# Pooled attention and a mixer on one core: K and Q turned by VectorE, maxima and diagonal Q moved by DMA

## The chip, the cores and the metric

The kernel runs on one core of one Trainium2 chip. The metric is the device time of one execution in microseconds (us). Before the change it is 923.01 us, the median of three runs (922.84 to 927.38).

## What is computed

Four batches of eight heads of attention, then a mixer over the result. The queries are averaged in pairs first, so each head has 576 pooled queries and 1152 keys of 64 numbers.

```python
q_pool = q.reshape(B, H, S // 2, 2, D).mean(axis=3)
scores = scale * np.matmul(q_pool, k.transpose(0, 1, 3, 2))
scores = scores - np.max(scores, axis=-1, keepdims=True)
attn = np.exp(scores)
attn = attn / (np.sum(attn, axis=-1, keepdims=True) + 1e-09)
x = np.matmul(attn, v)               # heads side by side: 4 x 576 x 512
h = np.maximum(x.T @ w_tok1, 0) @ w_tok2     # token mix, per batch
u = x + h.T
out = u + np.maximum(u @ w_ch1, 0) @ w_ch2   # channel mix
```

## The kernel before

Precision comes from splitting. [...] Everything is written as steps with a cost, a due time and buffers; a list planner (`Plan.run`) replays them on a model of the engines and so fixes, once, the order of each engine's instructions. The due times stand in the table `DUE`, in units of which one head has nine (`NS`), and `AFTER` and the cost functions are the planner's prices.

Work is done by pairs of heads, because two heads of 64 fill 128 partitions:

- `load_kq` loads K and Q of a pair (SP's queue): K as nine chunks into `KN`, Q with the two members of each pooled pair into `QN`. `prep_kq` adds the two members (`QP`, GpSimd or VectorE, L577) and turns K and Q by TensorE: three 128x128 turns for each of three K thirds (L588), three and two for Q (L614), into a slot of the PSUM ring `r` of three. ScalarE copies the rounded part out of the slot (`KHI`, L597; `QHI`, L628), VectorE subtracts it for the rest (`KLO`, L602; `QLO`, L638). ScalarE also copies the last 64 queries of each head into a diagonal tile `QD` (L634).
- `stack` puts, by DMA, the parts of one head on top of each other (`QQ`, `KK`, L666; `K2`, `Q2`, L671 and L674), so one 128-row matmul makes two of the products.
- `maxima` finds the row maximum of each query: twelve matmuls a head of 128 queries by 384 keys into a ring slot (L726) and a VectorE reduce each (L728), plus three a pair for the diagonal. A last reduce (L690) gives `MH`; TensorE turns it (L697), ScalarE copies it (`MT`, L699), and two DMAs write it as row 64 of `Q2` (L701, L704), so the scores matmul subtracts the maximum by itself.
- `main` runs nine steps a head: four scores matmuls of 288 columns (L792), two exponentials on ScalarE (`pf` in full at L807 into `PF`, rounded `ph` at L810), the rest `pl` on GpSimd or VectorE (L814), and PV matmuls (L839). In the heads of `IN_PV` (16 of 32) V has a 65th column of ones, so PV delivers the denominator and takes three matmuls a unit instead of two. The other heads add up `PF` on VectorE (L821) and turn the sums on TensorE (L885).
- `finish` turns the output of a head (L877), with 65 rows in `IN_PV` heads and 64 in the others, and scales it into `U` (L906).
- `token_mix` runs after every fourth head (L937, L955). After the last head the channel mixer `mm3`, `mm4` (L1052, L1080) runs with weights that `load_ch` narrowed from 64-bit words.

Tokens of K and V lie so that partition p holds tokens 9p to 9p+8 (`"(p c) d -> p c d"`); K's order within a head is free as long as V has the same.

Of the kernel before, what the change touches and what calls it, by code (L numbers as in the profile page):

```python
# [25 lines left out]
    (ACT, DVE): 131, (DVE, ACT): 128, (ACT, POOL): 159, (POOL, ACT): 75,  # L26
# [7 lines left out]
    "scores": -2.94,  # L34
    "p_lo": 5.94,
    "sum": -8.53,
    "pv": 1.65,
    "o": -51.23,
    "finish": 9.59,
    "max": -26.45,  # L40
    "max_each": 0.91,
    "prep": -32.39,
    "v": 3.41,
    "stack": 10.93,
    "stack_2": 29.0,
    "mix": 4.49,
    "mix_x": 5.65,
    "w_tok": 9.27,
    "w_tok_each": 4.51,
    "w_bits": -133.66,  # L50
    "sum_each": 0.15,
    "pv_lo": 0.35,
    "lo_first": -20.44,
# [40 lines left out]
IN_PV = (0, 1, 2, 3, 5, 8, 10, 13, 15, 19, 21, 24, 26, 28, 29, 31)  # L94
# [147 lines left out]
def kernel(  # L242
# [78 lines left out]
    def pool_(n):  # L321
        return 175 + 2.1 * n
# [101 lines left out]
    QP = early.tile([P, NQ, 2, D], F32, name="qp")  # L424
    VN = fix.tile([P, NK, D], F32, name="vn")
# [7 lines left out]
    MT = many(fix, 2, [NQ, P], F32, "mt")  # L433
# [8 lines left out]
    ve.memset(f(MH), 0.0)  # L442
# [3 lines left out]
    po.memset(PF[:, :, NK // 2, :, 1], 0.0)  # L446
# [28 lines left out]
    def tok_weights(after):  # L475
# [19 lines left out]
        for i, c, wh, wl in (  # L495
# [8 lines left out]
            for k, o in enumerate(  # L504
# [16 lines left out]
                step(POOL, 150 + 1.1 * m, lambda tmp=tmp: po.tensor_scalar(  # L521
# [24 lines left out]
    def load_kq(p, t, after):  # L546
        b, h0 = divmod(2 * p, H)

        def load_k(j, c0, c1):
            step(DMA, 2 * wire(4 * P * (c1 - c0) * D), lambda: sy.dma_start(  # L550
                KN[:, c0:c1, j], k[b, h0 + j].rearrange("(p c) d -> p c d", c=NK)[:, c0:c1]),
                t, write=[("kn", j, c) for c in range(c0 // 3, c1 // 3)], after=after)

        def load_q(j, c0, c1):
# [16 lines left out]
    def prep_kq(p, t):  # L571

        qh, ql = QHI[p % 2], QLO[p % 2]
        for i, (c0, c1) in enumerate(((0, 2), (2, 4), (4, 5))):
# [4 lines left out]
                t + due["q_pool"], [("qn", j, i // 2) for j in range(2)], [("qp", i)])  # L579
        tq = t - 1 if p == 0 else t + due["q_turn"]  # L580

        def keys(j):
# [3 lines left out]
            def turn(ps=ps, j=j):  # L586
                for c in range(3):
# [4 lines left out]
            step(PE, 3 * TURN, turn, t + j * due["k_each"], [("kn", 0, j), ("kn", 1, j)],  # L592
                 [ps, ("kh", j), ("kl", j)], [ps])
# [12 lines left out]
        def queries(i):  # L606
# [5 lines left out]
            def turn(ps=ps, c0=c0, c1=c1):  # L612
                for c in range(c0, c1):
# [4 lines left out]
            step(PE, (c1 - c0) * TURN, turn, tq + i,  # L618
                 [("qp", x) for x in ((0, 1) if i == 0 else (1, 2))],
                 [ps, ("qh", p % 2, i), ("ql", p % 2, i),  # L620
                  *(("qd", p % 2, x) for x in range(2 * i))], [ps])
# [55 lines left out]
    def maxima(h, t):  # L677
# [513 lines left out]
```

## Time and profile before

| | |
|---|---|
| median of three runs | 923.01 us |
| the profiled execution | 922.62 us |
| its span on the core | 920.8 us |
| TensorE busy, share of the span | 889.5 us, 97% |
| VectorE, ScalarE, GpSimd busy | 590.7, 562.1, 512.0 us |
| granted clock of TensorE, mean | 0.994 |
| DMA packets | 89686, 91.09 MB |

The span runs from the first to the last instruction; the rest of the execution's time lies around it. Busy times are unions of instructions, and matmuls overlap, so a busy TensorE is not one at its peak: the distance between starts says more. A line such as `L588 PE MATMUL r<-ident,kn 128*128 128x128 f32 x141 | 23.0, 275` would read: line 588, TensorE, writes `r` from `ident` and `kn`, 141 times, 23.0 us busy in all, 275 ns each; PEld is TensorE's weight load, DVE VectorE, ACT ScalarE, POOL GpSimd. Idle time and its releaser follow, where shown.

### The profile page before, as it was taken

What the parts mean: (1) busy time and instruction counts of PE and PEld (TensorE: products, weight loads), DVE (VectorE), ACT (ScalarE), POOL (GpSimd) and SP (SyncE); (2) the same over time, 40 slices, a digit from 0 to 9 for tenths busy, and PEclk for the clock granted to TensorE, in tenths of its full rate; (3) what the DMA queues carried; (4) which work ended last, traced back from release to release, by engine and by line L of the source; (5) the groups of instructions that cost most, each with busy time, mean ns of one, the idle gap of its engine ahead of it and who ended that gap; (6) DMA issues with size and microseconds to landing.
All of it is one profiled execution on the core that took longest, in us unless ns stands there. A gap on an engine that the chain in (4) does not pass through costs nothing.

```text
span 920.8 us, 15741 instructions
## 1 busy us (share of the span) xinstructions
PE 889.5 (97%) x5601; PEld 811.3 (88%) x5601; DVE 590.7 (64%) x1142; ACT 562.1 (61%) x1202; POOL 512.0 (56%) x414
## 2 busy tenths in 40 slices
PE   8899999999999999999999999999999999999997
PEld 6778889899989898999889999889989999998996
DVE  7567878887887689697888865778872222121211
ACT  5669889698788788798788979764431111111110
POOL 3679999797797698788688768643330000000000
PEclk9899999999999999999999999999999999999999
DMA  7778564565455555546634532133420101000001
GB/s 163 213 174 183 116 152 109 124 142 136 110 124 129 124 123 130 135 96 150 143 72 110 109 92 79 46 108 124 136 92 27 43 1 35 1 35 1 35 0 35
DMA packets 89686, 91.09 MB, mean 99 GB/s; under 512 B 43852, under 2 KB 68808, under 8 KB 89608
## 3 DMA queue, kind: packets, MB, share of 16 engines
q1 hardware_dynamic: 89608, 90.09, 39.9%
q8 instruction: 44, 0.72, 0.3%
q14 instruction: 34, 0.28, 0.1%
HBM read 43.25 MB, written 4.72 MB: 52 GB/s over the span
## 4 chain that ended last, share of the span: by engine, by line
PE 75%; ACT 10%; DVE 5%; issue 2%; DMA 1%; POOL 1%; SPq 0%; ACTq 0%; DVEq 0%; POOLq 0%
PE r L1052 17%; PE o L839 14%; PE s L1080 13%; PE s L792 12%; PE r L726 7%; ACT pf L807 3%; ACT ph L810 3%; PE o L1080 3%; PE r L937 2%; PE r L955 2%; PE r L877 2%; DVE mx L728 1%; PE r L885 1%; ACT u L906 1%; PE r L588 1%
## 5 line engine op out<-in xcount | busy, mean ns | idle before, releaser
L814 POOL TENSOR_TENSOR pl<-pf,ph 128x576 fp32r<-128x576 f32 x264 | 377.4, 1447 | 93.2 <-ACT pf L807 38.9
L728 DVE TENSOR_REDUCE mx<-r 128x1 f32<-128x384 f32 x384 | 197.4, 548 | 41.6 <-PE r L726 37.9
L810 ACT ACTIVATE ph<-s 128x576 fp32r<-128x576 f32 x288 | 187.6, 655 | 50.8 <-PE s L792 38.9
L807 ACT ACTIVATE pf<-s 128x576 f32<-128x576 f32 x288 | 194.2, 680 | 9.4 <-POOL pl L814 7.1
L839 PE MATMUL o<-ph,vv 128*65 128x288 f32 (+2 forms) x864 | 186.9, 302 | 3.9 <-ACT ot L846 1.4
L792 PE MATMUL s<-qq,kk 128*128 128x288 f32 x574 | 170.4, 309 | 5.6 <-ACT pf L807 5.3
L792 PE MATMUL s<-q,k 65*128 65x288 f32 x576 | 165.0, 298 | 1.4 <-ACT q L761 1.4
L1058 ACT ACTIVATE h<-r 128x384 fp32r<-128x384 f32 x72 | 35.3, 491 | 194.1 <-PE r L1052 194.0
L1060 DVE SCALAR_TENSOR_TENSOR h<-r,h 128x384 fp32r<-128x384 f32 x72 | 40.1, 556 | 169.0 <-ACT h L1058 168.8
L839 PE MATMUL o<-pl,vv 128*65 128x288 f32 (+1 forms) x576 | 135.7, 297 | 0.2 <-POOL pl L814 0.2
L839 PEld LDWEIGHTS o<-ph,vv 128*65 128x65 f32 (+2 forms) x864 | 125.7, 155 | 11.1 <-DVE ot L852 3.0
L726 PE MATMUL r<-kk,qq 128*128 128x384 f32 x372 | 127.1, 361 | 6.7 <-DMA q<-ql 1.2
L1080 PE MATMUL s<-w,h 128*128 128x512 f32 x504 | 130.8, 394 | 0.0
L792 PEld LDWEIGHTS s<-qq,kk 128*128 128x128 f32 x574 | 109.4, 191 | 14.9 <-ACT pf L807 12.3
L792 PEld LDWEIGHTS s<-q,k 65*128 65x128 f32 x576 | 110.1, 191 | 1.6 <-ACT q L761 1.6
L1052 PE MATMUL r<-big,w 128*128 128x384 f32 x576 | 109.0, 337 | 0.0
L821 DVE TENSOR_REDUCE sum<-pf 128x96 f32<-128x960 f32 x96 | 108.0, 1141 | 1.5 <-ACT pf L807 1.2
L1080 PEld LDWEIGHTS s<-w,h 128*128 128x128 f32 x504 | 93.4, 188 | 16.5
L1052 PEld LDWEIGHTS r<-big,w 128*128 128x128 f32 x576 | 101.7, 188 | 3.6 <-DVE big L1041 0.2
L839 PEld LDWEIGHTS o<-pl,vv 128*65 128x65 f32 (+1 forms) x576 | 88.1, 163 | 1.8 <-POOL pl L814 0.6
L726 PEld LDWEIGHTS r<-kk,qq 128*128 128x128 f32 x372 | 68.1, 189 | 19.2 <-DVE mx L728 4.6
L1015 POOL TENSOR_TENSOR w<-v,w 128x512 fp32r<-128x512 f32 x23 | 32.1, 1396 | 58.1 <-ACT w L1014 58.1
(131 smaller groups left out, 1168.5 us busy)
## 6 DMA issues: line engine op xcount, KB each, us to landing
raw<-in_moe_w_ch_dram SPq DMA_DIRECT2D x24, 512.0 KB, 3.6
kk<-kh SPq DMA_DIRECT2D x32, 288.0 KB, 6.2
qq<-qh SPq DMA_DIRECT2D x64, 144.0 KB, 3.0
kk<-kl SPq DMA_DIRECT2D x32, 288.0 KB, 4.2
vn<-in_v_dram SPq DMA_DIRECT2D x32, 288.0 KB, 2.6
k<-kk SPq DMA_DIRECT2D x31, 288.0 KB, 4.4
kn<-in_k_dram SPq DMA_DIRECT2D x30, 288.0 KB, 4.5
qn<-in_q_dram SPq DMA_DIRECT2D x32, 256.0 KB, 5.5
```

Source lines behind the costliest of these rows:

```text
L726: step(PE, mm(SP3), lambda ps=ps, w=w, x=x: te.matmul(at(ps)[:, 0:SP3], w, x, start=True, stop=True), t, read, [ps], [ps])
L728: step(DVE, dve(SP3), lambda ps=ps, m=m: ve.tensor_reduce(m, at(ps)[:, 0:SP3], axis=AX.X, op=ALU.max), t + due["max_of"], [ps], [key])
L792: te.matmul(at(st)[:, i, 0:HF], w[:, c * P:(c + 1) * P], x[:, fq * HF:(fq + 1) * HF], start=(n == 0), stop=(n == len(terms) - 1))
L807: step(ACT, act_ps(2 * HF) + (0 if near else 49), lambda pf=pf, st=st: sc.activation(pf, at(st)[:, :, 0:HF], AF.Exp, scale=ESC), t, [(st, ...
L810: step(ACT, act_ps(2 * HF), lambda ph=ph, st=st: sc.activation(at(ph), at(st)[:, :, 0:HF], AF.Exp, scale=ESC), t + due["p_hi"], [(st, 0), ...
L814: both(2 * HF, lambda e, pf=pf, ph=ph, pl=pl: e.tensor_sub(at(pl), pf, f(at(ph))), t + due["p_lo"], [("pf", s), ph], [pl], [pl], on=POOL i ...
L821: step(DVE, 65 + 1.06 * (NK + 1) * HF // CUT, lambda fq=fq, cs=cs: ve.tensor_reduce(SUM[:, fq, cs], PF[:, fq, :, cs].rearrange("p c x i -> ...
L839: lambda o=o, x=x, w=w, m=m, i=i, c=c, new=new, end=end: te.matmul(at(o)[0:m - w], VV[i2][:, c, w:m], at(x)[:, i], start=new, stop=end),
L1052: te.matmul(at(ps)[:, 0:GT], w[:, c], x[:, c], start=(c == 0 and n == 0), stop=(c == NC4 - 1 and n == 2))
L1058: step(ACT, act_ps(GT), lambda: sc.activation(at(h)[:, 0], at(ps)[:, 0:GT], AF.Relu), t, [ps], [h])
L1060: step(DVE, dve(GT), lambda: ve.scalar_tensor_tensor(out=at(h)[:, 1], in0=at(ps)[:, 0:GT], scalar=0.0, in1=f(at(h))[:, 0], op0=ALU.max, op ...
L1080: te.matmul(at(ps), a[:, x * P:(x + 1) * P], w, start=(fi == 0 and m == 0), stop=(fi == NF - 1 and m == 2))
```

## The change

For all pairs but the first:

- K and Q come as pieces of 32 floats (128 bytes), so that each 32 partitions hold one half of a head's 64 numbers, tokens by blocks of 32. VectorE then turns blocks of 32x32 within these partitions, 384 or 192 columns an instruction, straight into the ring slot. The TensorE turns of these pairs go. K and V have tokens in natural order now.
- The diagonal `QD` is copied by DMA from `QHI` instead of by ScalarE from PSUM.

For all heads: `MH` is written to the row of `Q2` by DMA as it is, 128 pieces of four floats, without TensorE's turn and ScalarE's copy; for that, a maxima matmul takes every fourth query (`c:4*P:4`) as its weights. V comes in nine pieces of 256 bytes a partition. Nineteen heads are in `IN_PV`. The output turn always has 65 rows. `PF` has ten slots in a row, five a half; slot numbers shift and nothing else. Many due times and some planner prices differ, so the order does too.

```diff
-    (ACT, DVE): 131, (DVE, ACT): 128, (ACT, POOL): 159, (POOL, ACT): 75,
+    (ACT, DVE): 131, (DVE, ACT): 128, (ACT, POOL): 235, (PE, POOL): 200, (POOL, ACT): 75,
...
-    "max_row": -47.64,
+    "max_row": -21.2,
...
-    "prep": -32.39,
+    "prep": -47.86,
...
+    "q_diag": -18.19,
...
-IN_PV = (0, 1, 2, 3, 5, 8, 10, 13, 15, 19, 21, 24, 26, 28, 29, 31)
+IN_PV = (0, 1, 2, 3, 5, 8, 10, 12, 13, 14, 16, 18, 21, 22, 23, 24, 26, 27, 31)
...
+    KBF = KN.rearrange("p c j d -> p (c j d)")
+    KB = KBF.rearrange("p (m i) -> p m i", i=32)
...
+        def load_k_blocks(j, y):
+            g = slice(64 * j + 32 * y, 64 * j + 32 * y + 32)
+            step(DMA, 2.1 * wire(4 * S * 32), lambda: sy.dma_start(
+                KB[g], k[b, h0 + j].rearrange("(m r) (y i) -> y r m i", r=32, y=2)[y]),
+                t, write=[("kn", j, c, y) for c in range(3)], after=after)
+
+        def load_q_blocks(j, y, x):
+            g = slice(64 * j + 32 * y, 64 * j + 32 * y + 32)
+            step(DMA, 2.1 * wire(4 * SQ * 32), lambda: sy.dma_start(
+                QB[g, x], q[b, h0 + j].rearrange("(m r x) (y i) -> x y r m i", r=32, x=2, y=2)[x, y]),
+                t, write=[("qn", j, y, x)], after=after)
...
+        for i, (o0, o1) in enumerate(((0, 384), (384, SQ)) if p else ()):
+            both(o1 - o0, lambda e, o0=o0, o1=o1: e.tensor_add(
+                QPB[:, o0:o1], QBF[:, 0, o0:o1], QBF[:, 1, o0:o1]), t + due["q_pool"],
...
+                step(DVE, 1.2 * SP3, lambda ps=ps, o=o: ve.transpose(
+                    bank(ps)[:, 0:SP3], KBF[:, o]), t + j * due["k_each"] + due["k_turn"], read,
+                    [ps, ("kh", j), ("kl", j)], [ps])
...
+                step(DVE, 1.2 * n, lambda ps=ps, o=o, n=n: ve.transpose(
+                    bank(ps)[:, 0:n], QPB[:, o]), tq + i, [("qp", i)], write, [ps])
...
+                        step(DMA, 100, lambda r=r, j=j: sy.dma_start(
+                            f(QD[p % 2])[r, j * REM:(j + 1) * REM], f(qh)[r, SQ - REM:SQ]),
+                             tq + 1.1 + due["q_diag"], [("qh", p % 2, 1)], [("qd", p % 2, j)])
...
-             lambda: sy.dma_start(vn, v[h // H, h % H].rearrange("(p c) d -> p c d", c=NK)),
+             lambda: sy.dma_start(vn, v[h // H, h % H].rearrange("(c p) d -> p c d", p=P)),
...
-        ps = Buf("r")
-        step(PE, 56, lambda: te.transpose(fr(at(ps))[:, 0:P], mh, identr), t,
-             ["mh"], [ps], [ps])
-        step(ACT, 158, lambda: sc.copy(mt, at(ps)[0:NQ, 0:P]), t, [ps], [("mt", h % 2)])
         row = f(Q2[h % 2])[D:D + 1]
-        step(DMA, 1, lambda: sy.dma_start(row[:, 0:4 * P], mt[0:4]), t,
-             [("mt", h % 2)], [("row", h % 2, c) for c in range(4)])
+        step(DMA, 300, lambda: sy.dma_start(
+            row[:, 0:4 * P].rearrange("o (p c) -> o p c", c=4), mh[:, 0:4]), t,
+            [("mh", 0)], [("row", h % 2, c) for c in range(4)])
...
-                w, x = QQ[i3][:, qc(c)], KK[i3][:, ks]
+                w, x = QQ[i3][:, c:4 * P:4], KK[i3][:, ks]
...
-        n = DT if pv else D
         for c in range(NQ):
             step(PE, 64, lambda c=c: te.transpose(
-                turned()[:, c, 0:n], ot[0:n, qc(c)], ident[0:n, 0:n]),
+                turned()[:, c, 0:DT], ot[0:DT, qc(c)], ident[0:DT, 0:DT]),
```

TensorE in the fifth head (head 4), where its output is turned for `finish`; `r` are ring slots, `ot` the output, `sum` the sums of float parts, `kn` the K of a later pair. Before:

```order
L588 MATMUL r_82<-ident,kn 128x128 x3
L726 MATMUL r_80<-kk_90,qq_95 128x384
...
L877 MATMUL r_81<-ident,ot_103 128x64
L885 MATMUL r_81<-ident,sum 128x128
L885 MATMUL r_82<-ident,sum 128x128 x4
L877 MATMUL r_81<-ident,ot_103 128x64 x4
L726 MATMUL r_80<-kk_90,qq_95 128x384
```

And now:

```order
L824 MATMUL s_78<-q_98,k_93 128x288
L870 MATMUL o<-ph_149,vv_119 65x288
L870 MATMUL o<-ph_149,vv_119 64x288 x2
L870 MATMUL o<-ph_149,vv_119 65x288
L907 MATMUL r_82<-ident,ot_103 128x65
L915 MATMUL r_82<-ident,sum 128x128
L907 MATMUL r_82<-ident,ot_103 128x65 x4
L915 MATMUL r_80<-ident,sum 128x128 x4
L870 MATMUL o<-pl_155,vv_119 65x288 x2
```

The turns of `kn` are gone from TensorE, and the output turns among the sum turns have 65 rows.

VectorE in the same heads: what stands around the K rests (`kl`). Before:

```order
L728 TENSOR_REDUCE mx_121<-r_80 128x1
L728 TENSOR_REDUCE mx_121<-r_81 128x1
L602 TENSOR_TENSOR kl<-r_82,kh 128x384
L728 TENSOR_REDUCE mx_121<-r_80 128x1
L814 TENSOR_TENSOR pl_158<-pf,ph_152 128x576
```

And now:

```order
L760 TENSOR_REDUCE mx_121<-r_82 128x1
L619 STREAM_TRANSPOSE r_82<-kn 128x384
L760 TENSOR_REDUCE mx_121<-r_80 128x1
L619 STREAM_TRANSPOSE r_80<-kn 128x384
L883 TENSOR_TENSOR ot_103<-o,low 64x288
L630 TENSOR_TENSOR kl<-r_82,kh 128x384
L630 TENSOR_TENSOR kl<-r_80,kh 128x384
```

Each K third now has two instructions on VectorE, the turn into the slot and the subtraction out of it, with ScalarE's copy between.

SP's queue, from one pair's loads to the maxima row of the next head (`q_98` is `Q2`; `mt` and `mh` the maxima). Before:

```order
L550 DMA kn<-in_k_dram 128x9x64 x2
L704 DMA q_98<-mt_123 1x16x4
L666 DMA qq_94<-qh_115 64x576 x2
L666 DMA kk_89<-kh 64x1152
L666 DMA kk_89<-kl 64x1152
L671 DMA k_93<-kk_91 64x1152
L674 DMA q_98<-ql_116 64x576
L701 DMA q_98<-mt_124 1x4x128
```

And now:

```order
L563 DMA kn<-in_k_dram 32x36x32 x4
L732 DMA q_98<-mh 1x128x4
L701 DMA kk_90<-kh 64x1152
L701 DMA kk_90<-kl 64x1152
L669 DMA qd_101<-qh_115 64x64 x2
L684 DMA vn<-in_v_dram 128x9x64
L569 DMA qn<-in_q_dram 32x18x32 x8
```

K and Q of a pair are twelve transfers where they were six, and they stand between the stacking transfers and the rows of the heads in work.

## Rows read from the trace of the kernel before

**Rows 1.** The page, part 1: busy us (share of the span) and instructions.

```profile
PE 889.5 (97%) x5601; PEld 811.3 (88%) x5601; DVE 590.7 (64%) x1142; ACT 562.1 (61%) x1202; POOL 512.0 (56%) x414
```

**Rows 2.** Windows: stretch, length, busy PE, PEld, DVE, ACT, POOL, granted clock, DMA share, GB/s.

```profile
0.00:100.00 100.00, 89.21 (x531) 73.79 (x532) 67.97 (x165) 69.64 (x152) 71.95 (x70) 0.97 0.74 179
100.00:575.00 475.00, 461.74 (x3275) 430.10 (x3273) 382.31 (x740) 400.77 (x864) 392.10 (x311) 1.00 0.52 119
...
621.00:920.00 299.00, 295.01 (x1509) 266.92 (x1508) 105.54 (x174) 59.23 (x116) 24.03 (x18) 1.00 0.14 44
```

**Rows 3.** The page, part 4: the chain that ended last, by engine.

```profile
PE 75%; ACT 10%; DVE 5%; issue 2%; DMA 1%; POOL 1%; SPq 0%; ACTq 0%; DVEq 0%; POOLq 0%
```

**Rows 4.** Waits, 100 to 580 us: who waited for whom, us, times, longest.

```profile
ACT ph L810 <- PE s L792: 35.0, 49, 3.1
DVE mx L728 <- PE r L726: 32.1, 49, 3.1
...
PEld s L792 <- ACT pf L807: 7.8, 18, 0.9
```

**Rows 5.** Timeline of PE at 234 us: start, us to the last end, instructions.

```profile
233.94 0.47 PE L877 MATMUL r<-ident,ot 65*128 65x65 f32 x5
...
234.57 0.43 PE L839 MATMUL o<-pl,vv 128*128 128x288 f32 x2
234.84 0.29 PE L792 MATMUL s<-qq,kk 128*128 128x288 f32 x1
```

**Rows 6.** Timeline of PE at 268 us, around three turns of K.

```profile
267.89 0.49 PE L588 MATMUL r<-ident,kn 128*128 128x128 f32 x3
268.13 0.38 PE L839 MATMUL o<-pl,vv 128*65 128x288 f32 x1
268.35 0.34 PE L726 MATMUL r<-kk,qq 128*128 128x384 f32 x1
268.52 0.29 PE L839 MATMUL o<-pl,vv 128*65 128x288 f32 x1
```

**Rows 7.** Timeline of PE at 243 us, around a turn of maxima.

```profile
243.32 0.22 PE L697 MATMUL r<-identr,mh 128*128 128x128 f32 x1
...
243.57 0.30 PE L792 MATMUL s<-q,k 65*128 65x288 f32 x1
```

**Rows 8.** Timeline of PE, two mixed turns of output and sums: first row, row after.

```profile
248.03 0.27 PE L877 MATMUL r<-ident,ot 64*128 64x64 f32 x1
...
249.88 0.30 PE L839 MATMUL o<-pl,vv 128*128 128x288 f32 x1
...
270.24 0.27 PE L877 MATMUL r<-ident,ot 64*128 64x64 f32 x1
...
271.75 0.29 PE L839 MATMUL o<-ph,vv 128*64 128x288 f32 x1
```

**Rows 9.** Groups by form, weight loads: count, busy us, mean ns, idle before and releasers.

```profile
L839 PEld LDWEIGHTS o<-ph,vv 128*128 128x128 f32 x288 | 50.0, 191 | 3.1 <-DVE ot L852 2.9
...
L839 PEld LDWEIGHTS o<-ph,vv 128*64 128x64 f32 x288 | 38.8, 135 | 1.6
```

**Rows 10.** Timeline of DVE at 245 us.

```profile
244.89 1.48 DVE L728 TENSOR_REDUCE mx<-r 128x1 f32<-128x384 f32 x3
246.28 0.44 DVE L852 TENSOR_TENSOR ot<-o,low 64x288 f32<-64x288 f32 x1
246.65 1.00 DVE L728 TENSOR_REDUCE mx<-r 128x1 f32<-128x384 f32 x2
```

**Rows 11.** Groups by form, DVE.

```profile
L821 DVE TENSOR_REDUCE sum<-pf 128x96 f32<-128x960 f32 x96 | 108.0, 1141 | 1.5 <-ACT pf L807 1.2
L814 DVE TENSOR_TENSOR pl<-pf,ph 128x576 fp32r<-128x576 f32 x24 | 23.7, 988 | 22.6 <-ACT ph L810 11.8 <-PE o L839 5.6 <-PE s L792 3.1
```

**Rows 12.** DMA issues by line: count, KB each, median us from issue to landing.

```profile
vn<-in_v_dram SPq DMA_DIRECT2D x32, 288.0 KB, 2.6
...
kn<-in_k_dram SPq DMA_DIRECT2D x30, 288.0 KB, 4.5
```

More of the change, by code (lines that the diff above doesn't have):

```diff
@@ L33 @@
 DUE = {
[L34 to L41, printed above, removed]
-    "prep": -32.39,
-    "v": 3.41,
-    "stack": 10.93,
-    "stack_2": 29.0,
+    "scores": -4.5,
+    "p_lo": 5.87,
+    "sum": -9.78,
+    "pv": 0.35,
+    "o": -76.73,
+    "finish": -37.65,
+    "max": -26.5,
+    "max_each": 0.65,
+    "prep": -47.86,
+    "v": 2.17,
+    "stack": 17.09,
+    "stack_2": 76.73,
     "mix": 4.49,
@@ new lines @@
+    "finish_each": -3.1,
+    "den_sum": -15.08,
+    "x_lo": -44.24,
+    "x": 27.99,
+    "den": -30.38,
+    "rd": -20.25,
+    "u": 23.45,
+    "u_each": -41.15,
+    "max_of": -11.3,
+    "max_row": -21.2,
+    "max_first_each": 11.02,
+    "q_pool": -54.73,
+    "q_turn": 5.19,
+    "k_each": 1.94,
+    "k_hi": 4.75,
+    "k_turn": -0.25,
+    "q_diag": -18.19,
+    "k_lo": -10.58,
+    "q_hi": -15.28,
+    "q_lo": -11.2,
+    "load_kq": -56.71,
+    "load_v": -34.48,
+    "v_lo": -62.7,
@@ L445 @@
     ve.memset(f(QD[1]), 0.0)
-    po.memset(PF[:, :, NK // 2, :, 1], 0.0)
+    for i in range(2):
+        po.memset(OT[i][D:DT], 0.0)
+    po.memset(PF[:, NK // 2:NK // 2 + 2, :, 1], 0.0)
     ve.memset(M0[:, 0:D], 0.0)
@@ L578, in prep_kq @@
                 QP[r, c0:c1], QN[r, c0:c1, :, 0], QN[r, c0:c1, :, 1]),
[L579 removed]
+                t + due["q_pool"], [("qn", j, i // 2, x) for j in range(2) for x in range(2)], [("qp", i)])
         tq = t - 1 if p == 0 else t + due["q_turn"]
@@ L590, in turn @@
                         KN[:, 3 * j + c].rearrange("p h d -> p (h d)"), ident)
-            step(PE, 3 * TURN, turn, t + j * due["k_each"], [("kn", 0, j), ("kn", 1, j)],
-                 [ps, ("kh", j), ("kl", j)], [ps])
+            read = [("kn", x, j, y) for x in range(2) for y in range(2)]
+            if p == 0:
+                step(PE, 3 * TURN, turn, t + j * due["k_each"], read, [ps, ("kh", j), ("kl", j)], [ps])
+            else:
+                step(DVE, 1.2 * SP3, lambda ps=ps, o=o: ve.transpose(
+                    bank(ps)[:, 0:SP3], KBF[:, o]), t + j * due["k_each"] + due["k_turn"], read,
+                    [ps, ("kh", j), ("kl", j)], [ps])
             if p == 0 and j == 0:
@@ L616, in turn @@
                         QP[:, c].rearrange("p h d -> p (h d)"), ident)
[L618 to L621, printed above, removed]
+            write = [ps, ("qh", p % 2, i), ("ql", p % 2, i), *(("qd", p % 2, x) for x in range(2 * i))]
+            if p == 0:
+                step(PE, (c1 - c0) * TURN, turn, tq + i,
+                     [("qp", x) for x in ((0, 1) if i == 0 else (1, 2))], write, [ps])
+            else:
+                step(DVE, 1.2 * n, lambda ps=ps, o=o, n=n: ve.transpose(
+                    bank(ps)[:, 0:n], QPB[:, o]), tq + i, [("qp", i)], write, [ps])
             if p == 0:
@@ L905, in finish @@
                             else (rows(4), 8, ("u8", b // 2, hh)))
-            step(ACT, 230 if c > 3 else 140, lambda c=c, r=r, row=row: sc.mul(
+            step(ACT, 200, lambda c=c, r=r, row=row: sc.mul(
                 u[r, row, col], turned()[r, c, 0:D], rd[r, c]),
```

116 lines of the change are left out of this document (49 added, 67 removed).

## The prediction, before the changed kernel ran

> **What bounds the kernel now.** I read the page first, for the load of each engine: TensorE is busy 97% of the span and nothing else is above 64% [rows 1]. That is an average over stages, so next come the stretches [rows 2]. From 621 us on TensorE runs without a hole (295 of 299 us) while VectorE, ScalarE and GpSimd are nearly empty. This is the channel mixer; the change puts no work on TensorE there and takes none away. From 100 to 575 us (the attention heads with the token mixes between them) TensorE is busy 462 of 475 us, VectorE 382, ScalarE 401, GpSimd 392, and the DMA engines half of the time. So the change must be priced in that stretch and in the 100 us before it, where TensorE has 11 us of holes and the DMA engines are at 0.74. The chain that ended last is 75% TensorE, 10% ScalarE and 5% VectorE [rows 3]. The waits say the same from the other side: in the middle stretch ScalarE waits 35 us for scores and VectorE 32 us for maxima matmuls, while the longest wait of TensorE's weight loads is 8 us [rows 4]. TensorE is the engine the others wait for, though not by much: three engines stand at 80 to 84%.
>
> A matmul's duration is mostly pipeline, so TensorE's work is priced by the distance from one start to the next. Two matmuls of the 288-column kind take 0.27 us from 234.57 to 234.84 [rows 5], 0.135 each; a maxima matmul of 384 columns takes 0.17 us, from 268.35 to 268.52 [rows 6].
>
> **The change, part by part: TensorE.**
> K and Q of 15 pairs are no longer turned there: 9 + 5 turns a pair, 210 in all. Three turns and one 288-column matmul stand between 267.89 and 268.35 [rows 6], 0.46 us; less 0.135 that is 0.325, or 0.108 a turn. 210 x 0.108 = **22.8 us less**.
> The maxima are no longer turned: 31 turns. One turn and one score matmul stand between 243.32 and 243.57 [rows 7], so a turn costs 0.115. 31 x 0.115 = **3.6 less**.
> Three more heads take their denominator as a 65th column of the PV matmul: 18 more matmuls each, 54 x 0.135 = **7.3 more**. Their 15 turns of sums go, 15 x 0.108 = **1.6 less**.
> In the 16 heads without that column, output turns of 64 rows now alternate with sum turns of 128 rows. Unmixed, five output turns of 65 rows cost 0.36 us (233.94 to 234.57 less two matmuls [rows 5]) and five sum turns 0.54, together 0.90. Mixed, ten turns with one maxima matmul take 1.85 us from 248.03 to 249.88, and 1.51 from 270.24 to 271.75 [rows 8]: less 0.17 that is 1.68 and 1.34, an excess of 0.78 and 0.44. Every output turn now has 65 rows. Between 16 x 0.44 = 7.0 and 16 x 0.78 = 12.5 I take 0.55 a head, **8.8 less**, nearer to the lower end because the longer one may hold a wait.
> The maxima matmuls now load their weights with a step of four elements, 372 of them. Before, no weight load has a step, so its price is bounded. A load of 128 columns lasts 191 ns and one of 64 lasts 135 [rows 9]: 0.87 ns a column, 112 ns of reading, hidden behind the 135 ns of the matmul ahead. Lower bound nothing. Upper bound: the reading doubles to 224 ns, 89 ns show, 372 x 0.089 = 33 us. I take nothing, since the nearest row, a load at 0.87 ns a column, already reads at half the pace of the matmul's moving side (135 ns for 288 columns), and both ends stay in the range.
> Sum: -22.8 - 3.6 - 1.6 - 8.8 + 7.3 = **29.5 us less on TensorE**.
>
> **The change: the other engines.** VectorE gets 60 block transposes of 384 columns and 15 of 192. The trace has none. The nearest rows are reduces of 384 columns, three in 1.39 us from 244.89 to 246.28 [rows 10], 0.463 each. Lower bound half of it, upper bound twice. I take 0.463 and 0.232, that is 27.8 + 3.5 = 31.3 us more. It loses 18 sum reduces at 1.14 [rows 11] and six additions at 0.37 (246.28 to the next start at 246.65 [rows 10]), 22.7 us; two small reduces in each of the three heads are left out of the account. The new order gives it six more subtractions of float parts at 0.99 [rows 11] and four of V, taken at the same price: 9.9. Net **+18.5**, 382 to 401 us. This costs nothing as long as TensorE is what the work waits for; where that cover goes is the second rival.
> ScalarE loses 31 copies of maxima and 30 of the diagonal, and GpSimd ten of those subtractions. Neither sets the end, so nothing is booked. The planner's due times put the transfers that replace the diagonal copies and the maxima's turn more than a head (nine units) ahead of their use, so a transfer's landing is covered by the heads between; nothing is booked for them either. If the queue were late by more than that, the third rival would show it. The layout of the float parts only renumbers slots: nothing.
> DMA: K goes from 2304 pieces a pair to 4608, Q from 1152 to 4608, V from 256 to 2304, the rows add some 400: 8200 more pieces with the same bytes. A K load lands 1.9 us later than a V load of the same 288 KB in a ninth of the pieces [rows 12]. Two K loads are issued back to back and delay each other, so I take half, 0.95 us for 1024 pieces: 7.6 us a pair, 114 us in all. Bounds: nothing, and twice that. SP issues 120 more transfers in the same queue, ahead of the stacking transfers of the next head; what that delays is part of the third rival.
>
> **From TensorE to the end.** Of 29.5 us, the chain's TensorE share of 75% [rows 3] comes off the end: 22.1 us. The rest becomes waits of TensorE for three engines that are then at 84 to 88%. The profiled execution took 922.6 us (span 920.8); 922.6 - 22.1 = 900.5. It is 0.4 below the median of the runs, so **901 us**. Full conversion gives 893, half of it 908.
>
> **The rivals.**
> First, the stepped weight load shows. At twice the reading time TensorE stands at -29.5 + 33 = +3.5 us, the end at 925; at one and a half times, 168 ns, 33 ns show, 372 x 0.033 = 12 us, the end at 922.6 - 0.75 x 17.5 = 909. For it: no load of the trace reads with a step, so nothing excludes it. Against it: the load is slow already, and some maxima matmuls follow one another, with 0.17 us to hide behind. [...]
> Second, VectorE becomes the bound, and the kernel gets slower. Without transposes VectorE's load in the stretch is 382 - 22.7 + 9.9 = 369 us. If it can be kept 88% busy, between ScalarE's 84% and TensorE's 97%, 475 us hold 418 us of it, so it decides from (418 - 369) / 75 = 0.65 us a transpose on. At twice my price (62.6 us) it has 432 us, needs 491, and the end goes to 939. For it: a transpose writes PSUM slots of the same ring of three that the maxima use. Against it: it would have to run at half the pace of every 384-column row of this engine.
> Third, small pieces delay the start. In the first 100 us the DMA engines have 26 us left; three pairs add 23. If a third of that becomes waiting, 8 us return: 909; if all, 924. For it: the 0.74 there [rows 2]. Against: after 100 us they idle half of the time. [...]
> Fourth, the change does not do what it says to the end: TensorE's freed time turns into waits for ScalarE and GpSimd, which keep their pace, and a quarter or less comes off: 917.
>
> **How the numbers follow.** Forecast 0.58 (893 to 908, predicted 901); stepped load 0.17 (909 to 925); VectorE 0.09 (930 to 939); small pieces 0.10 (909 to 924); no conversion 0.06 (917). A measurement here can tell 0.5%, 4.6 us, from no change: under 918.4 is faster, over 927.6 slower. Faster: 0.58, 0.08 of the stepped load, 0.07 of the small pieces, 0.03 of the last, 0.76. Slower: 0.09, and 0.02 for the stepped load beyond its upper bound, 0.11. Within: 0.13. The range from 889 to 924 leaves out the slow cases, 0.11, and 0.05 below for a schedule that also fills the first 100 us.
>
> **What would show it.** Right: the next matmul behind a maxima matmul still starts 0.17 us later; no turns by the K and Q lines on TensorE; output and sum turns together near 0.9 us a head; transposes near 0.46 us apart, with VectorE below 88%; the mixer after the attention as long as before (299 us). Wrong: maxima matmuls 0.2 us or more apart behind a score matmul with nothing waited for (first rival); ScalarE and TensorE waiting for VectorE's transposes (second); TensorE waiting for stacked K or Q in the first 100 us (third). An end at or above 918 us makes the prediction wrong.

## The result: the changed kernel took 931.2 us, 0.9% more than before

The median of five runs of the changed kernel is **931.2 us** (930.2 to 933.4), against 923.0 for the kernel before beside it: a ratio of 1.0086, 95% interval 1.0057 to 1.0116. The prediction was 901 us with a range of 889 to 924, and "faster" at 0.76. It was wrong in sign, and the time lies outside the range.

The profiled execution took 930.2 us, its span is 928.4. The page after, parts 1 and 4, answers to [rows 1, 3]:

```profile
span 928.4 us, 15308 instructions
PE 888.6 (96%) x5399; PEld 827.3 (89%) x5399; DVE 621.6 (67%) x1193; ACT 552.3 (59%) x1141; POOL 502.7 (54%) x394
PE 72%; DMA 9%; DVE 7%; ACT 6%; SPq 3%; issue 2%; POOL 1%; DVEq 0%; ACTq 0%; POOLq 0%
DMA packets 218348, 91.56 MB, mean 99 GB/s; under 512 B 194016, under 2 KB 201568, under 8 KB 218272
```

TensorE has 202 instructions fewer and is as busy as before; its weight loads are busy 16 us longer. DMA has gone from 1% of the chain to 9%. The stretches after, as in [rows 2]:

```profile
0.00:100.00 100.00, 81.45 (x439) 70.16 (x440) 71.36 (x168) 63.54 (x135) 69.34 (x67) 0.88 0.88 170
100.00:575.00 475.00, 462.68 (x3133) 444.16 (x3132) 403.04 (x780) 391.85 (x811) 378.85 (x288) 1.00 0.62 122
```

Two places stand out. In the first 100 us TensorE does 92 matmuls fewer than before (439 against 531), at a granted clock of 0.88 in place of 0.97. In the middle it is as busy as before with 142 instructions fewer, so each takes longer (0.148 us of busy time in place of 0.141).

**The middle: the maxima matmul.** Groups by form: the weight load before, then the weight load and the matmul after (the matmul had a mean of 361 ns before):

```profile
L726 PEld LDWEIGHTS r<-kk,qq 128*128 128x128 f32 x372 | 68.1, 189 | 19.2 <-DVE mx L728 4.6 <-issue 3.3 <-ACT u L906 2.8
L758 PEld LDWEIGHTS r<-kk,qq 128*128 128x128 f32 x372 | 112.6, 312 | 17.8 <-issue 6.0 <-DVE mx L760 3.0 <-DVE pl L845 1.6
L758 PE MATMUL r<-kk,qq 128*128 128x384 f32 x372 | 159.3, 448 | 9.7 <-DMA kk<-kl 8.2 <-DVE mx L760 0.8 <-DMA q<-ql 0.3
```

And the timeline of TensorE at 270 us, the same place as [rows 6]:

```profile
270.58 0.96 PE L758 MATMUL r<-kk,qq 128*128 128x384 f32 x3
271.38 0.29 PE L824 MATMUL s<-qq,kk 128*128 128x288 f32 x1
...
273.53 0.43 PE L758 MATMUL r<-kk,qq 128*128 128x384 f32 x1
273.80 0.29 PE L870 MATMUL o<-ph,vv 128*65 128x288 f32 x1
273.94 0.47 PE L907 MATMUL r<-ident,ot 65*128 65x65 f32 x5
274.22 0.32 PE L870 MATMUL o<-ph,vv 128*64 128x288 f32 x1
```

Three maxima matmuls one behind the other take 0.80 us, 0.27 each, and one alone takes 0.27 too, where [rows 6] had 0.17. Nothing is waited for. Over all 432 maxima matmuls of 384 columns (372 stepped, 60 not) the median distance to the next start is 0.275 us, before 0.178. Summed over the 372, the distances went from 79.5 to 109.9 us, 30.4 us more.

**The start.** TensorE's timeline at 37 to 49 us, after:

```profile
37.43 0.47 PE L907 MATMUL r<-ident,ot 65*128 65x65 f32 x4 [0.46 <-ACT ot L877]
47.87 0.66 PE L758 MATMUL r<-kh,qd 128*128 128x384 f32 x1 [9.98 <-DMA qd<-qh]
48.33 0.44 PE L824 MATMUL s<-qq,kk 128*128 128x288 f32 x1
48.57 0.44 PE L824 MATMUL s<-q,k 65*128 65x288 f32 x1
```

and that of SP's queue in the same stretch:

```profile
32.59 7.68 SPq L563 DMA_DIRECT2D kn<-in_k_dram  x4
40.38 4.70 SPq L569 DMA_DIRECT2D qn<-in_q_dram  x8
45.17 1.11 SPq L669 DMA_DIRECT2D qd<-qh  x2
46.32 0.59 SPq L732 DMA_DIRECT2D q<-mh  x1
```

TensorE waits 10 us for the diagonal Q of the second pair (pair 1), which is now a transfer. Its source, the copy on ScalarE, starts at 33.8. The transfer is issued at 45.2, because SP's queue first spends 12.4 us on the loads of pair 2 in 128-byte pieces. The transfer is what ended the wait, at 47.8 us, but not all that the matmul needed: it writes a slot of the ring `r`, and VectorE frees that slot with a subtraction that narrows the weights of the token mix:

```profile
44.66 0.42 DVE L543 TENSOR_TENSOR big<-r,big 128x256 fp32r<-128x256 f32 x1
```

With the diagonal Q there in time TensorE could have gone on at 45.1 us, 2.7 us earlier, and no more; the runs with the diagonal Q in time, below, show it. From 37.9 to 47.8 us TensorE starts nothing: the planner's order for the changed kernel puts nothing else ahead of this matmul. Windows of 23 us, before and after:

```profile
23.00:46.00 23.00, 19.69 (x112) 16.43 (x112) 12.10 (x30) 15.55 (x37) 15.96 (x15) 0.85 0.79 214
46.00:69.00 23.00, 20.84 (x132) 16.82 (x131) 16.04 (x39) 14.49 (x33) 18.32 (x16) 1.00 0.73 174
```

```profile
23.00:46.00 23.00, 13.49 (x84) 11.29 (x84) 16.53 (x41) 15.06 (x37) 18.19 (x15) 0.85 1.07 195
46.00:69.00 23.00, 17.85 (x80) 15.83 (x80) 16.89 (x40) 14.17 (x30) 15.72 (x14) 0.71 0.79 161
```

In the kernel before, TensorE is busy 19.7 us of the first of these and does 112 matmuls, and the second has a granted clock of 1.00. After the stall it is 0.71 (0.50 from 39 to 59 us), and scores matmuls start 0.24 us apart (48.33 to 48.57) where they took 0.135.

**Where the heads stand.** From the last scores matmul of each head in both traces: head 0 ends 6.5 us earlier than before, head 1 11.0 later, head 2 6.9 later, and head 31 6.6 later. The loss is made at the start. From head 2 on the two kernels run level: what TensorE was given there, something took back. From the last scores to the end both take 331 to 332 us, so the mixer is as long as before.

### The profile page after: what moved, and what is told of

It is laid out like the page before. It is cut to its first block, busy times and chain, and to the rows that moved or that the text cites. A ratio compares the mean times of both kernels' runs of the same rounds, so it can differ in the third digit from the quotient of the medians.

```text
span 928.4 us, 15308 instructions
## 1 busy us (share of the span) xinstructions
PE 888.6 (96%) x5399; PEld 827.3 (89%) x5399; DVE 621.6 (67%) x1193; ACT 552.3 (59%) x1141; POOL 502.7 (54%) x394
## 4 chain that ended last, share of the span: by engine, by line
PE 72%; DMA 9%; DVE 7%; ACT 6%; SPq 3%; issue 2%; POOL 1%; DVEq 0%; ACTq 0%; POOLq 0%
PE o L870 15%; PE r L1082 14%; PE s L824 12%; PE s L1110 11%; PE r L758 10%; DMA kk<-kl 5%; PE o L1110 2%; PE r L985 2%; DMA raw<-in_moe_w_ch_dram 2%; ACT pf L838 2%; ACT ph L841 2%; PE r L967 2%; DVE mx L760 1%; PE r L907 1%; DVE v L364 1%
## 5 line engine op out<-in xcount | busy, mean ns | idle before, releaser
L845 POOL TENSOR_TENSOR pl<-pf,ph 128x576 fp32r<-128x576 f32 x258 | 372.5, 1463 | 99.1 <-PE o L870 56.8
L760 DVE TENSOR_REDUCE mx<-r 128x1 f32<-128x384 f32 x384 | 199.4, 550 | 43.0 <-PE r L758 39.4
L870 PE MATMUL o<-ph,vv 128*65 128x288 f32 (+2 forms) x918 | 192.4, 299 | 3.4 <-DVE ot L883 1.7
L758 PE MATMUL r<-kk,qq 128*128 128x384 f32 x372 | 159.3, 448 | 9.7 <-DMA kk<-kl 8.2
L824 PE MATMUL s<-q,k 65*128 65x288 f32 x576 | 167.9, 301 | 0.3 <-ACT q L793 0.3
L870 PEld LDWEIGHTS o<-ph,vv 128*65 128x65 f32 (+2 forms) x918 | 132.4, 152 | 9.8 <-DVE ot L883 3.6
L758 PEld LDWEIGHTS r<-kk,qq 128*128 128x128 f32 x372 | 112.6, 312 | 17.8 <-issue 6.0
L824 PEld LDWEIGHTS s<-qq,kk 128*128 128x128 f32 x574 | 112.9, 197 | 10.2 <-ACT ph L841 6.0
L852 DVE TENSOR_REDUCE sum<-pf 128x96 f32<-128x960 f32 x78 | 88.1, 1135 | 4.6 <-ACT pf L838 4.5
```

What stands on the lines that cost most here:

```text
L758: step(PE, mm(SP3), lambda ps=ps, w=w, x=x: te.matmul(at(ps)[:, 0:SP3], w, x, start=True, stop=True), t, read, [ps], [ps])
L760: step(DVE, dve(SP3), lambda ps=ps, m=m: ve.tensor_reduce(m, at(ps)[:, 0:SP3], axis=AX.X, op=ALU.max), t + due["max_of"], [ps], [key])
L824: te.matmul(at(st)[:, i, 0:HF], w[:, c * P:(c + 1) * P], x[:, fq * HF:(fq + 1) * HF], start=(n == 0), stop=(n == len(terms) - 1))
L845: both(2 * HF, lambda e, pf=pf, ph=ph, pl=pl: e.tensor_sub(at(pl), pf, f(at(ph))), t + due["p_lo"], [("pf", s), ph], [pl], [pl], on=POOL i ...
L852: step(DVE, 65 + 1.06 * (NK + 1) * HF // CUT, lambda fq=fq, cs=cs: ve.tensor_reduce(SUM[:, fq, cs], PF[:, 5 * fq:5 * fq + 5, cs].rearrange ...
L870: lambda o=o, x=x, w=w, m=m, i=i, c=c, new=new, end=end: te.matmul(at(o)[0:m - w], VV[i2][:, c, w:m], at(x)[:, i], start=new, stop=end),
```

## The experiments

The theories, after the traces were read. **S**: the stepped weight load slows each maxima matmul, and this alone takes back the gain of the middle. **P** and **Q**: the 128-byte pieces occupy the DMA engines (P) or SP's queue (Q), and this makes the loss at the start. **W**: the new transfers (`qd`, the row of maxima) make the heads late. In each comparison the kernel before ran beside, at 921.6 to 923.0 us, so a difference from the changed kernel's 931.2 us carries an uncertainty of a microsecond or more.

**Neighbouring weights in the changed kernel.**

```
-                w, x = QQ[i3][:, c:4 * P:4], KK[i3][:, ks]
+                w, x = QQ[i3][:, qc(c)], KK[i3][:, ks]
```

> The changed kernel with one edit: the maxima matmuls take 128 neighbouring queries as weights again; the transfer of the row stays, so each row of scores is given the maximum of another query. The order on every engine is the same. Theory S (the stepped weight load eats what TensorE gained: in the changed kernel the distance behind a maxima matmul has a median of 227 ns, before 178, and 373 instead of 283 at the ninth tenth): the distance returns to 178 ns, 372 x 0.05 to 0.09 = 19 to 33 us of TensorE come back, and the time falls from 931 to about 911 (904 to 916). Rival V (the steady state is held by VectorE's transposes or by the small pieces): the load becomes shorter, but the time stays within 5 us of 931.

Measured 911.0 us, ratio to before 0.9883 (0.9854 to 0.9911), 20.2 us less than the changed kernel. The load, by form:

```profile
L758 PEld LDWEIGHTS r<-kk,qq 128*128 128x128 f32 x372 | 69.6, 191 | 27.6 <-issue 8.3 <-DVE mx L760 5.7 <-ACT u L936 2.0
L758 PE MATMUL r<-kk,qq 128*128 128x384 f32 x372 | 127.8, 360 | 13.8 <-DMA kk<-kl 11.0 <-DVE mx L760 1.2 <-DVE pl L845 0.9
```

The load is back at 191 ns and the median distance at 0.178 (in the changed kernel it is 0.275, not the 227 ns of the expectation). The stall of 10.3 us at the start stays. Head 1 ends 12.4 us late, and head 31 14.5 us early: the middle gains 27 us once the step is gone.

**The step in the kernel before.**

```
-                w, x = QQ[i3][:, qc(c)], KK[i3][:, ks]
+                w, x = QQ[i3][:, c:4 * P:4], KK[i3][:, ks]
```

> The kernel before with one edit: the maxima matmuls take every fourth query as weights; each row of scores is then given the maximum of another query. Theory S: the weight load grows from 189 to about 310 ns, the distance behind a maxima matmul by 50 to 90 ns, and the time by 19 to 33 us, to 942 to 956. Rival V (the load is hidden, or TensorE has room for it): within 4 us of 923.

Measured 943.3 us, ratio 1.0235 (1.0212 to 1.0257): 21.7 us more, with nothing else changed. The load takes 312 ns here too:

```profile
L726 PEld LDWEIGHTS r<-kk,qq 128*128 128x128 f32 x372 | 111.9, 312 | 13.0 <-DVE mx L728 2.6 <-ACT u L906 2.4 <-issue 2.1
```

Theory S holds from both sides, 20.2 and 21.7 us.

**The diagonal Q from ScalarE's queue.**

```
-                        step(DMA, 100, lambda r=r, j=j: sy.dma_start(
+                        step(DMA, 100, lambda r=r, j=j: sc.dma_start(
```

> The changed kernel with one edit: the transfers of the diagonal queries are issued from ScalarE's queue instead of SP's. Theory Q (in the first 50 us they stand in SP's queue behind 12 us of loads for the next pair, and TensorE stands still for 10 us, after which its clock is lower for a while): the stall is gone and the time falls by 8 to 11 us, to 920 to 923. Rival W (the DMA engines are full there, and the next transfer stalls instead): at most 3 us are won.

Measured 935.0 us, ratio 1.0139 (1.0117 to 1.0161): a miss. ScalarE issued the two transfers at 40.9 and 41.9 us, behind its other work. The stall became one of 7.2 us, and behind it one of 3.1 for the row of maxima, still in SP's queue behind the loads. The diagonal Q landed at 45.1 us, when VectorE freed the slot of the ring too. Another queue was no way past the loads here, since what it serves was itself in line.

**Both together, the row by single columns.** Weights as in the first, `qd` as in the third, and the row by four transfers of one column:

```
+            for c in range(4):
+                sy.dma_start(row[:, c * P:(c + 1) * P], mh[:, c:c + 1])
```

> The changed kernel with both edits, and with the row written by four transfers, one per column of maxima, so that each query has its own maximum. Theories S and Q together: 931 - 20 - 9 = 902 (895 to 908), faster than the kernel before by about 2%. Rivals V and W: 925 or more.

Measured 950.7 us, ratio 1.0327 (1.0293 to 1.0361): a miss by far. Waits of TensorE, 100 to 600 us:

```profile
PE r L761 <- DMA kk<-kl: 18.5, 13, 2.9
PE r L761 <- issue: 7.9, 4, 3.4
PE r L761 <- DMA qn<-in_q_dram: 5.5, 2, 2.9
```

From 100 to 575 us it has 17.3 us of the first; the changed kernel has 6.1 there, and neighbouring weights alone 8.7. Three more issues a head on SP fit the later stacking of the next head's K; this run changes three things (weights, queue of `qd`, row), so it does not show that alone.

**The loads in long pieces.** K in pieces of 4608 bytes, Q of 2304; bytes, number of loads and targets stay. The numbers land in other places within the targets, so the scores are not those of the reference: this run shows a cost, and is no version to use.

```
-                KB[g], k[b, h0 + j].rearrange("(m r) (y i) -> y r m i", r=32, y=2)[y]),
+                KBF[g], k[b, h0 + j].rearrange("(z r m) d -> z r (m d)", r=32, z=2)[y]),
...
```

> The changed kernel with the same number of K and Q loads, the same bytes and the same target partitions, but pieces of 4608 bytes (K) and 2304 bytes (Q) in place of 128; the tokens then lie scattered, so the scores are of other numbers. Theory P (the 128-byte pieces make pair 2's loads occupy SP's queue for 12 us and stall TensorE for 10 us at 38 us): the loads of pair 2 take SP under 8 us, the stall falls below 5 us, the DMA share from 100 to 575 us falls from 0.62 to under 0.55, and the time falls by 5 to 10 us, to 921 to 926. Rival O (it is the order: what a started head needs stands behind twelve loads, whatever their pieces): the stall stays within 2 us of 10, the time within 3 us of 931.

Measured 916.2 us, ratio 0.994 (0.9928 to 0.9952), 15.0 less than the changed kernel. The windows:

```profile
0.00:100.00 100.00, 86.65 (x473) 75.27 (x474) 76.51 (x179) 68.02 (x146) 73.77 (x71) 0.91 0.72 173
100.00:575.00 475.00, 468.20 (x3203) 451.89 (x3202) 408.32 (x789) 399.84 (x827) 384.45 (x292) 1.00 0.52 122
```

The gain is larger than theory P said, and two of its signs failed: the loads of pair 2 still take 8.9 us of SP, not under 8, and the stall is 6.5 us, not under 5. It now ends when VectorE frees the slot, at 44.2 us; the diagonal Q had landed at 42.9. The DMA share is back to what the kernel before has, 0.52. Head 1 ends 2 us earlier than in the changed kernel, head 2 6 earlier, head 31 14 earlier. So more than half of the price of the pieces is paid in the middle, a little in each head, where the prediction had booked none. There TensorE waited for stacked K; from 100 to 575 us, in the changed kernel and then here:

```profile
PE r L758 <- DMA kk<-kl: 6.1, 8, 1.3
PE r L758 <- DMA kk<-kl: 1.2, 1, 1.2
```

**The loads of pair 2 later.** They wait for the row transfer of the second head (head 1), and the planner orders anew.

```
...
+                    stacked if h == 2 else [rows_[1]] if h == 4 else ())
```

> The changed kernel with one edit: the loads of pair 2 wait for the transfer of head 1's maxima row, so that this row and the diagonal queries no longer stand behind them. The planner's order changes with it. Theory O (order in SP's queue): no stall over 4 us on TensorE between 30 and 60 us, head 1 ends its scores at 56 us or before in place of 65, and 6 to 11 us come off the end: 920 to 925. Rival W (the DMA engines are full there, and later loads stall pair 2 as long): at most 3 us come off, 928 or more.

Measured 926.4 us, ratio 1.0055 (1.0037 to 1.0073): 4.8 less than the changed kernel, between theory O and rival W, with no stall of 10 us, and head 1 only 4.4 us late. The new order also moves other steps, so the 4.8 us are not those of the loads alone.

**The maxima turned by TensorE again**, with neighbouring weights, alone and with the later loads:

```
+        step(PE, 56, lambda: te.transpose(fr(at(ps))[:, 0:P], mh, identr), t, ["mh"], [ps], [ps])
+        step(ACT, 158, lambda: sc.copy(mt, at(ps)[0:NQ, 0:P]), t, [ps], [("mt", h % 2)])
...
```

> The changed kernel with neighbouring queries as weights and the maxima turned by TensorE, copied by ScalarE and written by one transfer of four long pieces, as before the change. Theory S: 911 as with neighbouring weights alone, plus 31 turns at 0.115 us, 75% of it at the end: 914 (910 to 918), and every query with its own maximum. Rival V (what was won with neighbouring weights came from the mismatch of maxima or from the short chain of the row): 925 or more.

> The same as the kernel with turned maxima and neighbouring weights, and the loads of pair 2 wait for head 1's row. Theories S and O: 914 less 6 to 11, 903 to 908, about 2% below the kernel before. If W holds: 911 to 917.

Measured 931.1 us (ratio 1.0103, 1.0086 to 1.012) and 931.4 (1.0099, 1.0077 to 1.0122). Both missed. The added steps make the planner lay out another order, with due times that were set for other steps; waits of the first of the two, all engines, to 600 us:

```profile
POOL pl L849 <- ACT ph L845: 39.1, 16, 14.3
...
ACT mt L735 <- PE r L734: 15.0, 5, 6.4
```

A wait of 14.3 us is in neither of the kernels compared. These two runs say nothing of the step or of the turns.

**A step of two.** Weights of every second query, the row by two transfers of 8-byte pieces:

```
+                w, x = QQ[i3][:, c // 2 * 2 * P + c % 2:(c // 2 + 1) * 2 * P:2], KK[i3][:, ks]
...
+            for c in (0, 2):
+                sy.dma_start(row[:, c * P:(c + 2) * P].rearrange("o (p c) -> o p c", c=2), mh[:, c:c + 2])
```

> The changed kernel, with the maxima matmul's weights as every second query of a 256-query half (a step of 8 bytes) in place of every fourth (16 bytes), and the row of maxima put down by two transfers of 8-byte pieces. Theory N (what slows the weight load is the 16-byte step; at 8 bytes it goes as with neighbours): the load of the maxima matmul takes 189 ns again where the changed kernel's took 312, and the time is about 911 us (908 to 916), as with the neighbouring weights. Rival (any step slows the load, or the second row transfer costs SP's queue what the load gives back): 925 us or more, with the load well above 200 ns in the first case, and with it at 189 ns in the second.

Measured 921.1 us, ratio 0.999 (0.9968 to 1.0012), between the two. The load:

```profile
L761 PEld LDWEIGHTS r<-kk,qq 128*128 128x128 f32 x372 | 72.9, 201 | 37.2 <-issue 17.7 <-DVE mx L763 4.9 <-DVE mh L729 2.5
```

201 ns, and a median distance of 0.178 as with neighbours: a step of 8 bytes costs next to nothing, one of 16 bytes 0.12 us a load. (The medians of the load are 188 ns with neighbours, 196 and 309.) But 10 of the 20 us did not come. TensorE's waits for stacked K (`kk<-kl`) in the middle are 15.4 us, where the changed kernel has 6.1 and neighbouring weights 8.7, and what differs from the latter beside the step is the second row transfer in SP's queue. That it is the cause was not shown by itself. The profiled execution was a long one, 928.0 us; the same kernel with moved loads, below, has 14.4 us of these waits in one of 918.9.

**The loads of pair 2 moved in SP's queue alone**, to behind the row transfer of head 1, with the step of two and with that of four:

```
...
+        rest = [s for s in order if s not in pair_2]
+        i = rest.index(rows_[1]) + 1
+        for s in rest[:i] + [s for s in order if s in pair_2] + rest[i:]:
```

> As f1_step2, and the loads of pair 2's K and Q stand in SP's queue behind the row transfer of the second head instead of ahead of it; nothing else changes place. Theory Q (the stall of 10 us near 38 to 48 us is SP's queue, which issues these twelve loads for 12 us while the two transfers that TensorE needs stand behind them): the stall goes, and the time is 899 to 908 us, about 903. Rival (the loads, 12 us later, are then late for the turns of pair 2, so the wait only moves): 909 to 916 us, as f1_step2.

> The changed kernel with that move of the loads in SP's queue alone, the weights still every fourth query. Theory Q: the stall of 10 us goes, and the time is 922 to 925 us, some 6 to 9 us less than the changed kernel. Rival (the wait only moves to the turns of pair 2): 928 us or more.

Measured 921.5 us (ratio 0.9994, 0.9972 to 1.0015) and 930.1 (1.0084, 1.0058 to 1.0111): neither differs from its kernel without the move. The second kernel: the longest of TensorE's waits in the first 120 us, then the issue of the diagonal Q on SP, the subtraction on VectorE, and the matmul that waited:

```profile
PE r L758 <- DMA qn<-in_q_dram: 6.8, 1, 6.8
...
35.41 1.11 SPq L669 DMA_DIRECT2D qd<-qh  x2
...
45.15 0.42 DVE L543 TENSOR_TENSOR big<-r,big 128x256 fp32r<-128x256 f32 x1
...
45.63 0.69 PE L758 MATMUL r<-kh,qd 128*128 128x384 f32 x1 [6.75 <-DMA qn<-in_q_dram]
```

There was no gain, as the rival said, but not for its reason. The profile puts the wait down to a load of Q; yet the matmul reads K and diagonal Q of pair 1, and the load is pair 2's. The diagonal Q landed at 40.9 us. What ended last is VectorE's subtraction, at 45.58, and the matmul starts 0.05 us behind it, as with the long pieces (44.24 and 44.29). So the wait was for the slot of the ring, which no move of a load frees. The granted clock falls as before: 0.88 over the first 100 us, as in the changed kernel. Theory Q is out as it stood: the loads ahead in SP's queue hold the diagonal Q up, but getting it 7 us earlier is worth about 1 us at most. Rival W is out for the start with it, since the row of maxima was early too; for the middle the runs with more row transfers leave it open. Of P it holds that the pieces cost time, 15.0 us, but not in the way that it gave. No run moved the narrowing of these weights alone, so what the rest of the stall costs is open.

**65-row turns in the kernel before.**

```
-        n = DT if pv else D
+        n = DT
```

> The kernel before, with every turn of an output tile on 65 rows instead of 128; nothing else. The term of the prediction's sum for it (16 heads by 0.55 us, at three quarters on the path): 5 to 9 us less, 914 to 918 us. Rival (the gap beside 128-row turns is hidden by other waits of TensorE): within 2 us of 923.

Measured **914.8 us**, ratio 0.9914 (0.9894 to 0.9935): 8.1 us less than before, from one line. The term of the prediction for it was 8.8 us on TensorE. The ten turns that begin [rows 8], up to the next matmul, before and here:

```profile
248.03 0.27 PE L877 MATMUL r<-ident,ot 64*128 64x64 f32 x1
...
249.60 0.44 PE L726 MATMUL r<-kk,qq 128*128 128x384 f32 x1
```

```profile
248.51 0.22 PE L877 MATMUL r<-ident,ot 65*128 65x65 f32 x1
...
249.57 0.42 PE L726 MATMUL r<-kk,qq 128*128 128x384 f32 x1
```

1.57 us became 1.06. In the four heads where only one sum turn stands beside the output turns, 0.85 us became 0.39. This version leaves nothing of the work out and beats both kernels.

**Neighbouring weights and long pieces; neighbouring weights and later loads.** The edits shown above, two at a time.

> The changed kernel with both edits at once: neighbouring weights in the maxima matmul (a row gets another query's maximum) and the loads in long pieces (its tokens stand in another order). Alone the first took 20.2 us off 931.2 and the second 15.0. Theory A (the forecast's sum was right but for two things it booked at nothing, the stepped weight load and the 128-byte pieces, and these lie in different places): the gains add, 893 to 901 us, at or a little below the forecast of 901. Rival (both free the same waits, or another limit such as VectorE stands just behind): 904 to 911 us, little under the neighbouring weights alone.

> The changed kernel with neighbouring weights (a row gets another query's maximum) and with the loads of pair 2 waiting for the row transfer of the second head. Alone the first took 20.2 us off 931.2 and the second 4.8. Theory A: the gains add, 904 to 908 us. Rival: within 2 us of 911.

Measured **892.2 us**, ratio 0.9671 (0.9657 to 0.9685), and 907.9 us, 0.9842 (0.9825 to 0.986). The gains add: 931.2 - 20.2 - 15.0 = 896.0, and 4 us more came; 931.2 - 20.2 - 4.8 = 906.2. The middle stretch of the first, with 191 matmuls more than the changed kernel in the same time:

```profile
100.00:575.00 475.00, 463.11 (x3324) 436.30 (x3323) 412.47 (x811) 409.65 (x859) 395.75 (x301) 1.00 0.53 123
```

That is the forecast of 901 less 9: with the two costs taken out that the forecast booked at nothing, the rest of its sum is there, and VectorE at 412 of 475 us is no limit yet. TensorE's waits for stacked K are 1.5 us in this stretch, 8.7 with neighbouring weights alone. The stall at the start is there, 6.5 us, and head 1 is 7.2 us late. Neither kernel is a version to use: a softmax may subtract any number, but one that belongs to another query does not guard its exponential, and with the long pieces the scores are not those of the reference.

## Why the prediction was wrong, point by point

**The step that failed first: "The maxima matmuls now load their weights with a step of four elements ... I take nothing".** The bounds were 0 and 33 us, and the upper one was nearly it. The load went from 189 to 312 ns, 0.12 us more, the median distance to the next start from 0.178 to 0.275, and the 372 distances together from 79.5 to 109.9 us. With these 30.4 us the sum on TensorE is -29.5 + 30.4 = +0.9 us: the forecast's gain is gone, and at three quarters the end is at 923.3. The one edit that takes the step out or puts it in is worth 20.2 and 21.7 us. The reason given ("already reads at half the pace of the matmul's moving side") compared two reads that go side by side (weight loads busy 88% of the span, matmuls 97% [rows 1]); how long one load lasts with a step does not follow from it. The first rival had this mechanism and its price, 925 us, at a chance of 0.17. No row of before has a load with a step, so that chance was the author's estimate; the runs give the price: neighbours 191 ns, a step of 8 bytes 201, one of 16 bytes 312.

**The second: the 128-byte pieces at no cost on the path.** The prediction booked 7.6 us a pair on the DMA engines and nothing at the end. The pieces together cost 15.0 us (long pieces), or 18.8 (with neighbouring weights in both: 911.0 - 892.2). By the ends of the heads, 6 to 8 us of it are there at head 2 and 8 to 10 come after, spread over the heads; TensorE's waits for stacked K, 6.1 and 8.7 us without the long pieces and 1.2 and 1.5 with them, are most of the latter. Here the third rival came true beside the first: its price, 8 to 23 us, was right, and so were the busy DMA engines (0.88 over the first 100 us, 1.07 in 23 to 46). Its place was right in part, since it looked at the first 100 us alone.

**The third, with a small price: the diagonal Q and the rows "more than a head (nine units) ahead of their use".** The due times are a plan in steady state. At pair 1 there are no heads ahead: the diagonal Q was ready at 34, issued at 45, used at 48. This is the wait of 10 us in the trace, but 2.7 us of it at most are the transfer's; behind it stood the slot of the ring, and with the diagonal Q early the time fell by about 1 us at most. That the planner's new order leaves TensorE without work beside the narrowing of the token-mix weights is a cost that no term and no rival had. A lower clock went with it (0.71 in 46 to 69 us).

The rivals were priced as alternatives. Both happened: 901 + 20.2 + 15.0 is 936, 5 us over the 931.2 measured.

**What held.** The turns off TensorE, the 65-row turns and the wider PV: with both costs out, 892.2 us, which is "full conversion gives 893". So close a match is in part luck: of its terms only the 65-row turns were measured alone, the start is still late, and the long pieces are longer than those of the kernel before. The factor of 0.75 was too cautious in that direction: 8.1 of 8.8 us for the 65-row turns alone, and 30.8 of 29.5 in all. Against the step it was a little high: 20.2 of 30.7 us, and 21.7 of 31.1 in the kernel before. In the changed kernel ten mixed turns without a wait take 0.78 to 1.0 us, near the 0.9 that was to be seen. The fourth rival (no conversion) is out.

**VectorE.** Its transposes, after, by form:

```profile
L619 DVE STREAM_TRANSPOSE r<-kn 128x384 f32<-128x384 f32 x45 | 25.7, 581 | 1.8 <-DMA kn<-in_k_dram 1.5
L651 DVE STREAM_TRANSPOSE r<-qp 128x192 f32<-128x192 f32 x15 | 5.6, 375 | 0.1
...
249.71 0.58 DVE L619 STREAM_TRANSPOSE r<-kn 128x384 f32<-128x384 f32 x1
250.21 0.43 DVE L995 TENSOR_TENSOR u<-r,u 128x256 f32<-128x256 f32 x1
```

From 249.71 to 250.21, 0.50 us, near the 0.463 taken. VectorE went from 382 to 403 us in the middle (401 forecast). ScalarE waited 5.1 us in all for its transposes and GpSimd 3.6, which the forecast had at nothing; no matmul of TensorE waited for one in the middle, and with 412 us of VectorE the kernel still took 892.2: the second rival is out.

**The output turns** stand 0.06 us apart, 0.28 for five (273.94 to 274.22 in the timeline at 270 us). They did so before: the timeline that [rows 5] are from has the next matmul at 234.22, 0.28 behind the first turn, so the prediction's 0.36 holds 0.08 us of the two matmuls that follow. Its mixed turns hold some of the next matmul too: 1.57 and 1.26 us, not 1.68 and 1.34. The two readings about cancel, and the excess stays 0.75 and 0.44.

## What to carry to other kernels

An unknown cost in an instruction that runs hundreds of times next to the bound is the forecast: with bounds of 0 and 33 us around a sum of -29.5, the two ends are two forecasts, and the choice needs a measured row, not a likeness. Before a transfer replaces a copy, read its queue at the first place where it is used, not in steady state, and count the issue time of what stands ahead of it. A wait is put down to what ended last: before you remove that, look when everything else that the instruction needs was there, a free buffer above all. Rivals that lie in different places add; price them together as well as apart.

## What the runs showed of the hardware

- TensorE's weight load of 128x128 4-byte elements: neighbours 189 to 191 ns in the mean, step of 8 bytes 201, step of 16 bytes 312, and the step of 16 bytes shows in the distance of matmuls, 0.275 us against 0.178.
- Turns of 64 rows next to turns of 128 cost 8 us in 16 heads; 65 rows instead of 64, more work by count, took that away (914.8 us against 922.9; ten turns 1.06 us in place of 1.57).
- One stall of 10 us near the start went with a granted clock of 0.71 from 46 to 69 us, and one of 6.5 us (neighbouring weights and long pieces) with 0.78; the kernel before, with no such stall, had 1.00 there.
- The same bytes in 128-byte pieces cost 15 to 19 us of this kernel against pieces of 2304 and 4608 bytes. SP was held 2.5 to 7.7 us by four K loads in 128-byte pieces; for pair 2 it was 7.7 us, and 2.0 us by the same in 4608, with its Q loads 12.4 and 8.9 us.
